# Transposes of the attention stage on 64 lanes at a time, moved in between the third and the last scores

## The chip, the cores and the metric

The kernel runs on one core of a Trainium2 chip. The metric is the device time of one execution in microseconds (us), lower is better. The program of before ran three times; the median of these is the time that the change is compared with. One more execution was taken by the hardware profiler; all views of the trace come from it.

## What is computed

Three stages follow each other, in float32. Attention with a sigmoid in place of the softmax, on 4 x 12 heads of 448 tokens with 64 features; then two MLPs over all 1792 tokens (768 features, 2048 hidden ones), the first with ELU between its products, the second with h - tanh(h).

```python
def _attn_ref(q, k, v):                       # (4, 12, 448, 64) each
    scores = scale * np.matmul(q, k.transpose(0, 1, 3, 2)) - np.log(S)
    attn = 1.0 / (1.0 + np.exp(-scores))
    return np.matmul(attn, v).astype(np.float32)
...
    x = attn_out.transpose(0, 2, 1, 3).reshape(B * S, H * D)
    h = x @ w_in;  g = np.where(h > 0, h, np.exp(np.minimum(h, 0)) - 1);  x = g @ w_out
    h = x @ moe2_w_in;  return (h - np.tanh(h)) @ moe2_w_out
```

The four weights lie in memory as pairs of 32-bit words (float64). They are loaded whole and narrowed on the chip by one ScalarE pass (L538) and two VectorE passes (L541, L545).

## The kernel before

**Stages.** Attention takes about the first 180 us, the two MLPs the rest. The MLPs form their products out of seven block products instead of eight (L743 the first matrix of each MLP, L898 the second); for this the weights need sums of their blocks. The output weights of the first MLP are read, narrowed and summed already during attention, in eight pieces j = 0 to 7 of two 768 KB loads each (`p_load`, L589), which land in two rooms, XA and XB, used in turn by j odd and even; `p_narrow` (L593), `p_sum` (L596) and `p_store` (L600) then take each piece on to a scratch in DRAM, `p_forms`. In the trace of L538 the tile names XA and XB show such a piece. Three quarters of the input weights' pieces are loaded in the same time (`job`, L1030 on).

**Attention.** The 48 heads go in 24 pairs. For a pair n:
- `ld_qk` (L221) loads q and k, `side_by_side` (L226, GpSimd) copies them so that the two heads' features lie side by side in 128 columns. Tokens lie on the partitions (lanes): k in chunks of 128 tokens, q in chunks of 112.
- `transpose(n, w)` (L296) turns the four chunks of k (w=1) and of q (w=0) on TensorE, into the two halves (PSUM banks) of one PSUM tile called `sps`. Features of head 0 then lie on lanes 0 to 63, of head 1 on lanes 64 to 127.
- `head` (L305) copies the turned values to `e`, rounded to fp32r, k on ScalarE, q on VectorE; `rest` (L313, VectorE) writes what the rounding left. Two buffers of `e` (`es`) serve even and odd pairs.
- `scores(n, u)` (L326), u = 0 to 3, are the products for four blocks of key tokens. For u < 3 the two heads run in two halves of the TensorE array, 64 lanes each, six matmuls into one `sps` tile; u = 3 takes 128 lanes at once (both heads' last 64 keys), three matmuls into a tile of its own, `spq`.
- `sig(n, u)` (L346, ScalarE L352) takes the sigmoid of each; `pv(n, u)` (L356, TensorE L363) multiplies by v into `pvps`; `xdone` (L368, VectorE L375) stores the result.

There are three `sps` tiles. Scores u = 0 to 2 of a pair and the transposes for the pair two later share them in rotation: the transposes of pair n + 2 run in the turn of pair n, into the tile that the scores (n, 0) used, so they wait for the sigmoid (n, 0).

**Order.** A scheduler in the kernel (`Sched`) sets the order of every engine. Attention's operations stand at times of a table, `PHASES`, one turn of `CYCLE` = 6900 per pair, and go onto their engines in that order. A first pass plans the operations of attention alone; the second fits all others (narrowing, sums, x forms, here "fill-in work") on ScalarE and VectorE into the gaps: one may start when it ends no more than `GIVE` = 100 ns after the planned start of the next attention operation on its engine. All loads and stores of this stage but a few at the start are issued by one engine, SyncE (SP), in order.

Of the kernel before, what the change touches and what calls it, by code (L numbers as in the profile page):

```python
# [13 lines left out]
ALU = mybir.AluOpType  # L14


class Sched:
# [1 line left out]


    def __init__(self):
        self.ops, self.before, self.plan = {}, {}, {}
# [8 lines left out]
    def emit(self, only_plan=False):  # L31
        ops, plan, late = self.ops, self.plan, 0

        planned = {q: sorted((k for k in plan if ops[k][0] == q), key=plan.get, reverse=True) for q in ("ACT", "DVE")}
        after = {k: [a for a in o[3] if a in ops] for k, o in ops.items()}
        then = {k: [] for k in ops}
        left = {}
        for k, a in after.items():
            a = set(a) | ({self.before[k]} if k in self.before else set())
            left[k] = len(a)  # L40
            for x in a:
                then[x].append(k)
        ready, free, done, order = {}, {}, {}, []
        for k, n in left.items():
            if not n:
                ready.setdefault(ops[k][0], {})[k] = 0
        while any(ready.values()):
            best = None
            for queue, keys in ready.items():
                t0 = free.get(queue, 0)  # L50
                for k, t in keys.items():
                    c = (max(t, t0), ops[k][4], str(k))
                    if k not in plan and planned.get(queue) and c[0] + ops[k][1] > plan[planned[queue][-1]] + late + GIVE:
                        c = (10 ** 9,) + c[1:]
# [12 lines left out]
            for x in then[k]:  # L67
                left[x] -= 1
                if not left[x]:
                    ready.setdefault(ops[x][0], {})[x] = max((done[y] for y in after[x]), default=0)  # L70
        assert len(order) == len(ops)
        if only_plan:
            self.plan = {o[3]: o[0] for o in order}
# [26 lines left out]
def kernel(  # L100
# [20 lines left out]
    nc = tc.nc  # L121
# [3 lines left out]
    R = 4  # L125
# [17 lines left out]
    def f(ap):  # L143
        return ap.bitcast(F32)
# [23 lines left out]
    with tc.manual_schedule():  # L168
# [7 lines left out]
        def attention():  # L176
# [18 lines left out]
                base=0, channel_multiplier=1,  # L195
            )

            DD = 2 * D
            raw_qk = ld_p.tile([128, 4 * NL * R * D], F32, name="raw_qk")

            def parted(t):
                a, b = NL * R * DD, NL * (R + 3) * DD
                return t[:SP, :a], t[:, a:b], t[:, b:b + NL * DD].rearrange("p (i x) -> p i x", i=NL)

            (ql, kl, rest0), (qraw, kraw, rest1) = parted(first), parted(raw_qk)
            krest = rest0, rest1
# [2 lines left out]
            vl = [vs_p.tile([128, NL, 10, D], F32, name=f"vl{i}") for i in range(NVL)]  # L209

            es = [e0, ld_p.tile([128, 4, 512], F32R, name="e1")]
            for i in range(2):
                nc.gpsimd.memset(krest[i][RS:128, :, :D], 0.0)
                nc.gpsimd.memset(krest[i][0:RS, :, D:], 0.0)
# [3 lines left out]

            T = {}

            def ld_qk(w, n):  # L221
                b, hp = pairs[n]
                x = k[b, 2 * hp:2 * hp + 2, 0:384].rearrange("h (p c) d -> p h (c d)", c=3) if w else q[b, 2 * hp:2 * hp + 2].rearrange("h (p r) d -> p h (r d)", r=R)
# [14 lines left out]
            def ld_first(kind, i):  # L238

                b, hp = pairs[i]  # L240
                h = slice(2 * hp, 2 * hp + 2)
                if kind == "k":
                    nc.sync.dma_start(out=kl[:, i].rearrange("p c (h d) -> p c h d", h=2), in_=k[b, h, 0:384].rearrange("h (p c) d -> p c h d", c=3))
                else:
                    (nc.sync if i else nc.scalar).dma_start(out=ql[:, i].rearrange("p c (h d) -> p c h d", h=2), in_=q[b, h].rearrange("h (p r) d -> p r h d", r=R))

            def ld_v(m, i):
                by = nc.sync if m or i else nc.scalar
# [19 lines left out]
            def loads(m):  # L268
# [11 lines left out]
                for x, (kind, args) in enumerate(jobs):  # L280
                    free = {"k": (2, ("t", 1)), "q": (2, ("t", 0)), "v": (NVL, ("pv", 3))}[kind[0]]
                    last = [(free[1][0], NL * (m - free[0]) + i) + free[1][1:] for i in range(NL)]
                    sch.op(
                        ("ld" + kind, m) + args, "SP", 600 * {"kfirst": 1, "qfirst": 1, "kr": 2, "v": 1, "vr": 2}[kind],
                        lambda kind=kind, args=args: kinds[kind](m, *args),
                        last, when("ldv" if kind[0] == "v" else "ldk", NL * m) + x, 2500,
                    )
# [6 lines left out]
                return [part] + ([("ldkr", m)] if kind == "k" else [])  # L294

            def transpose(n, w):  # L296
                if ("tps", n) not in T:
                    T["tps", n] = pss[(4 * n - 5) % 3].tile([128, 2, BK], F32, tag="s", name="sps")
                T["t", n, w] = ps = T["tps", n][:, w]
                P, t = ((SP, ql), (128, kl))[w]  # L300
                for c in range(R):
                    x = krest[n // NL % 2][:, n % NL] if w and c == 3 else t[:, n % NL, c]
                    nc.tensor.transpose(ps[:, c * P:(c + 1) * P], x, ident[:P, :P])  # L303

            def head(n, w):  # L305
                W, slot = ((S, 1), (512, 2))[w]
                to, x = es[n % 2][:, slot, :W], T["t", n, w][:, :W]
                if w:
                    nc.scalar.activation(out=to, in_=x, func=ACTF.Copy)
                else:  # L310
                    nc.vector.tensor_copy(out=to, in_=x)  # L311

            def rest(n, w):  # L313
                W, slot, to = ((S, 1, 0), (512, 2, 3))[w]
                e = es[n % 2]
                nc.vector.tensor_tensor(
                    out=e[:, to, :W], in0=T.pop(("t", n, w))[:, :W], in1=f(e[:, slot, :W]), op=ALU.subtract
                )

            def keep_warm(n):  # L320
# [66 lines left out]
            for n in range(NPR):  # L387
# [4 lines left out]
                used = [("s", n - 2, u) for u in range(4)]  # L392
                for w in (1, 0):
                    if n >= NL:
                        sch.op(("ldqk", n, w), "SP", 600, lambda n=n, w=w: ld_qk(w, n), [("side", n - NL, w)], when("ldqk", n) - w, 5000)
# [16 lines left out]
        def mlp():  # L412
# [617 lines left out]
            def job(key, keeps, place, after=(), only=False, i=0):  # L1030
# [7 lines left out]
                after = list(after) + list(stage_frees[place])  # L1038
                if not live:
                    after.append(("keep", kept_by[key], key))  # L1040
                raw_op(("load", n), "SP", 600, lambda: load(n, key, not live), after, 8500 if place == 4 else 8500 if live else 6000)
                done = ("load", n)
                if place == 4:
                    fixed[done] = 3 * CYCLE + n
# [9 lines left out]
                stage_frees[place] = [done]  # L1054
                if keeps:
                    kept_by[key] = n
                    raw_op(("keep", n, key), "SP", 600, lambda: keep(n, key), [done], 12000 if place == 4 else 5600)
# [319 lines left out]
            for j in range(NG):  # L1377
# [97 lines left out]
```

## Time and profile before

| | us |
|---|---|
| median of three runs (lowest, highest) | 1003.37 (1001.11, 1007.04) |
| profiled execution, its own time | 1005.48 |
| its span in the profile | 1003.70 |
| TensorE busy in the span | 989.4 |
| attention, up to the last turn of pairs | about 180 |

The mean granted clock of TensorE in the profiled execution is 0.996 of full speed. A timeline groups neighbouring instructions of one kind: start, length of the whole group, line, tile, count, and in square brackets the idle time of the engine just before the group and what ended it. Matmuls are pipelined, so a group's length overlaps with the next one's start by some tens of nanoseconds; the distance between starts is the safer number. Lane counts stand as "lanes*columns" of the stationary operand.

### The profile page before, as it was taken

What the parts mean: (1) busy time and instruction counts of PE and PEld (TensorE: products, weight loads), DVE (VectorE), ACT (ScalarE), POOL (GpSimd) and SP (SyncE); (2) the same over time, 40 slices, a digit from 0 to 9 for tenths busy, and PEclk for the clock granted to TensorE, in tenths of its full rate; (3) what the DMA queues carried; (4) which work ended last, traced back from release to release, by engine and by line L of the source; (5) the groups of instructions that cost most, each with busy time, mean ns of one, the idle gap of its engine ahead of it and who ended that gap; (6) DMA issues with size and microseconds to landing.
All of it is one profiled execution on the core that took longest, in us unless ns stands there. A gap on an engine that the chain in (4) does not pass through costs nothing.

```text
span 1003.7 us, 15632 instructions
## 1 busy us (share of the span) xinstructions
PE 989.4 (99%) x5294; PEld 854.3 (85%) x5294; DVE 765.2 (76%) x1155; ACT 600.6 (60%) x966; POOL 105.2 (10%) x118
## 2 busy tenths in 40 slices
PE   8999999999999999999999998999999999999998
PEld 5655565788888888888899987888988999999998
DVE  2798777988888888668887898877777789665673
ACT  4778668766666666656566564444444555446652
POOL 2111210202222220000000201111111000000000
PEclk9999899999999999999999999999999999999999
DMA  8999950155555579999984734555555894455442
GB/s 258 286 356 343 328 180 27 48 192 190 187 188 191 192 254 323 396 364 389 377 284 128 243 90 156 181 196 190 185 188 186 308 330 148 127 170 174 130 144 86
DMA packets 144751, 218.61 MB, mean 218 GB/s; under 512 B 21600, under 2 KB 103072, under 8 KB 144416
## 3 DMA queue, kind: packets, MB, share of 16 engines
q1 hardware_dynamic: 143120, 217.04, 63.8%
q8 instruction: 41, 0.67, 0.3%
q10 hardware_dynamic: 1552, 0.59, 0.2%
q14 instruction: 38, 0.31, 0.1%
HBM read 142.61 MB, written 74.97 MB: 217 GB/s over the span
## 4 chain that ended last, share of the span: by engine, by line
PE 95%; DMA 2%; DVE 1%; ACT 1%; issue 0%; SPq 0%; ACTq 0%; DVEq 0%
PE psa L743 12%; PE psd L743 11%; PE psx L743 10%; PE pvps L363 7%; PE psu L898 7%; PE psw L898 7%; PE psv L898 7%; PE psa L898 6%; PE psb L898 6%; PE psb L743 5%; PE sps L338 5%; PE psy L898 5%; PE psx L898 3%; PE sps L303 2%; PE spq L338 2%; PE psd L898 1%
## 5 line engine op out<-in xcount | busy, mean ns | idle before, releaser
L352 ACT ACTIVATE an<-sps,bias 128x896 f32<-128x896 f32 x72 | 67.5, 1006 | 38.1 <-PE sps L338 38.0
L870 ACT ACTIVATE XB<-t 128x384 fp32r<-128x384 f32 (+1 forms) x111 | 61.9, 562 | 36.5 <-PE psw L898 8.4
L874 DVE TENSOR_TENSOR XB<-t,XB 128x384 fp32r<-128x384 f32 (+1 forms) x111 | 68.1, 624 | 11.4 <-ACT XB L870 11.2
L658 POOL TENSOR_TENSOR second<-second 128x384 f32<-128x384 f32 x15 | 18.9, 1263 | 539.9 <-DMA t<-x_forms 213.5
L363 PE MATMUL pvps<-an,vl 128*64 128x448 f32 x288 | 61.7, 565 | 0.0
L870 ACT ACTIVATE XB<-spare 128x512 fp32r<-128x512 f32 (+1 forms) x72 | 40.9, 573 | 26.4 <-PE psw L898 11.4
L338 PEld LDWEIGHTS sps<-e 64*128 64x128 f32 x432 | 39.7, 190 | 19.7 <-PE pvps L363 15.5
L743 PE MATMUL psa<-XB,W 128*128 128x512 f32 x192 | 54.2, 391 | 0.0
L338 PE MATMUL sps<-e 64*128 64x448 f32 x432 | 52.2, 384 | 0.0
L874 DVE TENSOR_TENSOR XB<-spare,XB 128x512 fp32r<-128x512 f32 (+1 forms) x72 | 44.0, 621 | 7.7 <-ACT XB L870 7.4
L898 PE MATMUL psu<-XB,XB 128*128 128x384 f32 (+1 forms) x192 | 46.3, 348 | 0.0
L898 PE MATMUL psw<-XB,XB 128*128 128x384 f32 (+1 forms) x192 | 46.2, 348 | 0.0
L898 PE MATMUL psv<-XB,XB 128*128 128x384 f32 (+1 forms) x192 | 46.2, 348 | 0.0
L743 PEld LDWEIGHTS psa<-XB,W 128*128 128x128 f32 x192 | 36.0, 188 | 7.6
L363 PEld LDWEIGHTS pvps<-an,vl 128*64 128x64 f32 x288 | 19.0, 140 | 27.3 <-issue 21.0
L772 ACT ACTIVATE spare<-t 128x512 f32<-128x512 f32 (+1 forms) x33 | 19.1, 579 | 37.1 <-DVE t L760 35.9
L658 POOL TENSOR_TENSOR first<-first,second 128x384 f32<-128x384 f32 x30 | 40.0, 1333 | 1.2
L228 POOL COPY first<-raw_qk 128x384 f32<-128x384 f32 (+1 forms) x44 | 26.0, 599 | 122.6 <-DMA raw_qk<-in_k_dram 69.9
L311 DVE CAST e<-sps 128x448 fp32r<-128x448 f32 x24 | 15.0, 625 | 29.7 <-PE sps L303 22.6
L743 PE MATMUL psd<-XB,W 128*128 128x512 f32 x144 | 35.7, 391 | 1.5 <-DVE W L675 1.3
L776 ACT ACTIVATE spare<-spare 128x512 f32<-128x512 f32 (+1 forms) x64 | 36.7, 573 | 0.7
L898 PE MATMUL psa<-XB,XB 128*128 128x384 f32 (+1 forms) x156 | 36.9, 347 | 0.0
(363 smaller groups left out, 2759.1 us busy)
## 6 DMA issues: line engine op xcount, KB each, us to landing
x_forms<-R1b SPq DMA_DIRECT2D x58, 256.0 KB, 2.0
first<-p_forms SPq DMA_DIRECT2D x36, 384.0 KB, 6.6
t<-x_forms SPq DMA_DIRECT2D x64, 192.0 KB, 3.0
t<-x_forms SPq DMA_DIRECT2D x47, 256.0 KB, 4.9
x_forms<-t SPq DMA_DIRECT2D x44, 256.0 KB, 2.0
x_forms<-R1b SPq DMA_DIRECT2D x58, 192.0 KB, 4.9
first<-in_moe_w_in_dram SPq DMA_DIRECT2D x14, 768.0 KB, 5.4
second<-in_moe_w_in_dram SPq DMA_DIRECT2D x14, 768.0 KB, 6.7
```

The lines of the kernel that those rows point to most:

```text
L228: nc.gpsimd.tensor_copy(out=(ql, kl)[w][:, n % NL].rearrange("p c (h d) -> p c h d", h=2), in_=x)
L303: nc.tensor.transpose(ps[:, c * P:(c + 1) * P], x, ident[:P, :P])
L338: nc.tensor.matmul(out=ps[:, j, :S], lhsT=e[lanes, ks, cols], rhs=e[lanes, qs, :S], start=(x == 0), stop=(x == 2),)
L352: nc.scalar.activation(out=a[:, :m], in_=T.pop(("s", n, u))[:, :m, :S], func=ACTF.Sigmoid, bias=bias, scale=scale)
L363: nc.tensor.matmul(out=ps[D * j:D * j + D], lhsT=vl[n // NL % NVL][:, n % NL, 5 * j + u if u < 3 else 3 + j], rhs=a[:, j if u < 3 else 0], ...
L658: by.tensor_tensor(out=out, in0=x, in1=y, op=op)
L743: nc.tensor.matmul(out=ps, lhsT=w[wz][:, k0:k0 + 128], rhs=xs[xz][:, kk], start=(opens and n == 0), stop=(n == 3 * KH - 1), skip_group_che ...
L772: nc.scalar.activation(out=r, in_=h, func=ACTF.Tanh)
L776: nc.scalar.activation(out=r, in_=r, func=ACTF.Exp, scale=-1.0)
L870: nc.scalar.activation(out=at_place(og_place[i, s, p, j], 0, i)[:, :HW[s]], in_=T["graw", i, s, p, j], func=ACTF.Copy)
L874: nc.vector.tensor_tensor(out=lo, in0=T.pop(("graw", i, s, p, j)), in1=f(hi), op=ALU.subtract)
L898: nc.tensor.matmul(out=T["o2", tag], lhsT=lhsT, rhs=rhs, start=(p in OPENS and j == 0 and x == 0), stop=(j == NG - 1 and x == 2), skip_gro ...
```

## The change

The transposes take half of the lanes each: for k two of 64 lanes per chunk, for q two of 56 (at lanes 0 and 64), the two halves into the two PSUM banks; 16 instead of 8 for a pair, each with half as many moving columns. They are emitted between the third scores and the last, not after the last. `head` and `rest` read the turned values by a strided view of the two banks. q is loaded in two transfers per pair, not one, since its tokens now start at lanes 0 and 64, and the GpSimd copy takes 120 lanes. In the scheduler, fill-in work may end later than the next planned operation's start, by 100 ns or 0.4 of that operation's slack; the lateness that it allows for is TensorE's alone. Two rules set when the weights' loads may be issued: piece j of the output weights after the first scores of pair 16 * j // 10 (before: of pair 1 for all), and the input weights' first pieces after scores (0, 1).

```diff
-                    if k not in plan and planned.get(queue) and c[0] + ops[k][1] > plan[planned[queue][-1]] + late + GIVE:
+                    if k not in plan and planned.get(queue) and c[0] + ops[k][1] > self.until[planned[queue][-1]] + late:
...
-                late = start - plan[k]
+                if queue == "PE":
+                    late = start - plan[k]
...
+                last = min([ends[x] - (wait if k in after[x] else cost) for x in then[k]], default=plan[k])
+                ends[k] = plan[k] if ops[k][0] == "PE" else max(plan[k], last)
+            self.until = {k: plan[k] + max(GIVE, int(SLACK * (ends[k] - plan[k]))) for k in plan}
...
+SLACK = 0.4
...
-    ("s", 0): 0, ("s", 1): 620, ("s", 2): 1240, ("s", 3): 1900,
-    ("t", 1): 3100 - 2 * CYCLE, ("t", 0): 3500 - 2 * CYCLE, ("pv", 0): 4000, ("pv", 1): 4900, ("pv", 2): 5800, ("pv", 3): 6500,
+    ("s", 0): 0, ("s", 1): 620, ("s", 2): 1240, ("s", 3): 2400,
+    ("t", 1): 1900 - 2 * CYCLE, ("t", 0): 2100 - 2 * CYCLE, ("pv", 0): 4000, ("pv", 1): 4900, ("pv", 2): 5800, ("pv", 3): 6500,
...
-                nc.sync.dma_start(out=(qraw, kraw)[w][:, n % NL], in_=x)
...
+                for a in range(2):
+                    nc.sync.dma_start(out=qraw[64 * a:64 * a + SH, n % NL], in_=q_rows(b, h, a).rearrange("h (p r) d -> p h (r d)", r=R))
...
-                P, t = ((SP, ql), (128, kl))[w]
+                ps = T["tps", n]
+                P, t, c0 = ((SH, ql, 256), (64, kl, 0))[w]
                 for c in range(R):
                     x = krest[n // NL % 2][:, n % NL] if w and c == 3 else t[:, n % NL, c]
-                    nc.tensor.transpose(ps[:, c * P:(c + 1) * P], x, ident[:P, :P])
+                    for a in range(2):
+                        lanes = slice(64 * a, 64 * a + P)
+                        nc.tensor.transpose(ps[:, a, c0 + c * P:c0 + (c + 1) * P], x[lanes], ident[lanes, lanes])
+                T["t", n, w] = ps[:, :, c0:c0 + R * P].rearrange("p a (c x) -> p c a x", c=R)
...
-                    op("t", n, (w,), "PE", (420, 440)[w], transpose, loaded("qk"[w], n) + before_s(n - 2, 3))
+                    op("t", n, (w,), "PE", (250, 280)[w], transpose, loaded("qk"[w], n) + before_s(n - 2, 3))
...
-                    op("p_load", (j, c), "SP", 600, p_load, [("s", 1, 0)] + (was[c:c + 1] if wide else held), 11000)
+                    op("p_load", (j, c), "SP", 600, p_load, [("s", 0 + 16 * j // 10, 0)] + (was[c:c + 1] if wide else held), 11000)
```

**On TensorE**, one turn in the middle of attention. L338 are the scores (L364 after the change), L303 the transposes (L328), L363 the products with v (L389); e_120 and e_83 are the two buffers of `e`. Before:

```order
L338 MATMUL sps<-e_120 128x448 x18
L338 MATMUL spq<-e_120 128x448 x3
L303 MATMUL sps<-ident,first 128x128 x3
L303 MATMUL sps<-ident,raw_qk 128x128
L303 MATMUL sps<-ident,first 128x112 x4
L363 MATMUL pvps<-an,vl_118 64x448 x6
L363 MATMUL pvps<-a,vl_118 64x448 x2
```

After the change:

```order
L364 MATMUL sps<-e_120 128x448 x18
L328 MATMUL sps<-ident,first 128x64 x6
L328 MATMUL sps<-ident,raw_qk 128x64 x2
L328 MATMUL sps<-ident,first 128x56 x8
L364 MATMUL spq<-e_120 128x448 x3
L389 MATMUL pvps<-an,vl_118 64x448 x6
L389 MATMUL pvps<-a,vl_118 64x448 x2
```

The transposes have moved ahead of the last scores, and there are twice as many with half the columns. The order of the MLPs' instructions is the same on all engines.

**On ScalarE**, the place where piece 5 of the output weights is narrowed (XB_71<-XA_70). L352 are the sigmoids (L378 after), L309 the rounding of k (L337), L709 the forms of x (L735). Before, the last row is the first three sigmoids of pair 12:

```order
L352 ACTIVATE an<-sps,bias 128x896 x3
L352 ACTIVATE a<-spq,bias 128x448
L309 ACTIVATE e_120<-sps 128x512
L538 ACTIVATE XB_71<-XA_70 128x768 x2
L709 ACTIVATE XA<-R0b 128x512
L352 ACTIVATE an<-sps,bias 128x896 x3
```

After the change, the last row is the first three sigmoids of pair 11:

```order
L378 ACTIVATE an<-sps,bias 128x896 x3
L378 ACTIVATE a<-spq,bias 128x448
L337 ACTIVATE e_83<-sps 128x512
L564 ACTIVATE XB_71<-XA_70 128x768 x2
L378 ACTIVATE an<-sps,bias 128x896 x3
```

Piece 5 is narrowed one turn earlier, and a form of x has left that gap. Pieces 4 and 6 move by one turn as well (now ahead of pairs 9 and 13); piece 7 stands ahead of pair 15 in both.

**On SyncE's queue**, around the loads of the same piece (XA_70<-in_moe_w_out_dram; L589, L615 after). L224 loads q and k of a pair (L240 and L243 after), L603 and L629 store sums, L557 keeps a narrowed input weight in DRAM. Before:

```order
L603 DMA p_forms<-XB_71 128x384
L589 DMA XA_70<-in_moe_w_out_dram 128x1536
L557 DMA kept_wi_3_872<-R1b 128x768
L603 DMA p_forms<-XB_71 128x2x384
L233 DMA raw_qk<-in_k_dram 64x2x64 x2
L224 DMA raw_qk<-in_k_dram 128x2x192
L224 DMA raw_qk<-in_q_dram 112x2x256
L589 DMA XA_70<-in_moe_w_out_dram 128x1536
```

After the change:

```order
L273 DMA vl_119<-in_v_dram 128x2x192
L240 DMA raw_qk<-in_k_dram 128x2x192
L629 DMA p_forms<-XB_71 128x2x384
L243 DMA raw_qk<-in_q_dram 56x2x256 x2
L615 DMA XA_70<-in_moe_w_out_dram 128x1536 x2
L629 DMA p_forms<-XB_71 128x4x384
```

The two loads of the piece stand together, and each load of q is two. Up to and with the second of these loads SyncE issues 103 transfers instead of 95, and 26.38 MB instead of 27.26 MB.

## Rows read from the trace of the kernel before

**Rows 1.** The page: busy time of each engine, and its DMA share by slices.
```profile
PE 989.4 (99%) x5294; PEld 854.3 (85%) x5294; DVE 765.2 (76%) x1155; ACT 600.6 (60%) x966; POOL 105.2 (10%) x118
...
DMA  8999950155555579999984734555555894455442
```

**Rows 2.** Timeline of TensorE, one turn with transposes: start, length, instructions.
```profile
66.83 2.09 PE L338 MATMUL sps<-e 64*128 64x448 f32 x18
...
68.56 0.37 PE L338 MATMUL sps<-e 64*128 64x448 f32 x2
...
68.85 0.89 PE L338 MATMUL spq<-e 128*128 128x448 f32 x3
69.59 0.49 PE L303 MATMUL sps<-ident,first 128*128 128x128 f32 x3
...
70.02 0.55 PE L303 MATMUL sps<-ident,first 112*128 112x112 f32 x4
70.50 2.48 PE L363 MATMUL pvps<-an,vl 128*64 128x448 f32 x12
...
73.66 0.47 PE L338 MATMUL sps<-e 64*128 64x448 f32 x2
```

**Rows 3.** Timeline of TensorE, the last turns, which have no transposes.
```profile
167.94 2.09 PE L338 MATMUL sps<-e 64*128 64x448 f32 x18
...
173.93 0.47 PE L338 MATMUL sps<-e 64*128 64x448 f32 x2
```

**Rows 4.** Timeline of ScalarE in the turn of rows 2.
```profile
67.81 2.81 ACT L352 ACTIVATE an<-sps,bias 128x896 f32<-128x896 f32 x3 [0.60 <-PE sps L338]
...
74.63 1.01 ACT L352 ACTIVATE an<-sps,bias 128x896 f32<-128x896 f32 x1 [1.41 <-PE sps L338]
```

**Rows 5.** Timeline of TensorE around its longest stop.
```profile
119.84 1.83 PE L303 MATMUL sps<-ident,first 128*128 128x128 f32 x8 [2.39 <-ACT an L352]
...
127.03 2.09 PE L338 MATMUL sps<-e 64*128 64x448 f32 x18
```

**Rows 6.** Timeline of ScalarE ahead of that stop.
```profile
117.39 0.89 ACT L538 ACTIVATE XB<-XA 128x768 f32<-128x768 f32 x1 [2.87 <-DMA XA<-in_moe_w_out_dram]
118.70 2.79 ACT L352 ACTIVATE an<-sps,bias 128x896 f32<-128x896 f32 x3
```

**Rows 7.** The chain that ended last, from 104 to 119 us: start, length, what.
```profile
108.58 8.73 DMA XA<-in_moe_w_out_dram
```

**Rows 8.** Windows: stretch, length, busy PE, PEld, DVE, ACT, POOL, clock, DMA share, GB/s.
```profile
28.00:32.00 4.00, 4.00 (x27) 2.35 (x27) 1.63 (x3) 3.87 (x6) 0.68 (x2) 1.00 0.77 208
36.00:40.00 4.00, 4.00 (x25) 1.74 (x25) 3.52 (x7) 3.88 (x6) 1.39 (x2) 1.00 0.62 187
60.00:80.00 20.00, 20.00 (x137) 12.19 (x135) 18.07 (x29) 16.63 (x22) 3.49 (x6) 1.00 1.01 340
119.40:126.20 6.80, 6.36 (x22) 3.05 (x24) 2.44 (x4) 3.85 (x6) 2.18 (x4) 0.50 1.03 327
```

**Rows 9.** Weight loads by line and shape: count, busy us, mean ns of one, idle.
```profile
L338 PEld LDWEIGHTS sps<-e 64*128 64x128 f32 x432 | 39.7, 190 | 19.7 <-PE pvps L363 15.5 <-issue 1.3 <-DVE e L316 0.4
...
L338 PEld LDWEIGHTS spq<-e 128*128 128x128 f32 x72 | 11.9, 191 | 8.0 <-issue 7.6
```

**Rows 10.** Timeline of TensorE at the first turn.
```profile
13.04 1.11 PE L338 MATMUL spq<-e 128*128 128x448 f32 x3
...
15.45 0.57 PE L303 MATMUL sps<-ident,first 112*128 112x112 f32 x4 [0.86 <-ACT e L309]
15.96 2.48 PE L363 MATMUL pvps<-an,vl 128*64 128x448 f32 x12
...
19.12 1.08 PE L338 MATMUL sps<-e 64*128 64x448 f32 x8
```

**Rows 11.** Timeline of SyncE's queue: start, time to issue, what.
```profile
70.82 0.38 SPq L224 DMA_DIRECT2D raw_qk<-in_q_dram  x1
...
85.39 0.53 SPq L589 DMA_DIRECT2D XA<-in_moe_w_out_dram  x1
```

**Rows 12.** The load issued at 85.39, by its source line.
```profile
DMA to landing us min/median/max: 7.4/7.4/7.4
```

More of the change, by code (lines that the diff above doesn't have):

```diff
@@ L21, in __init__ @@
     def __init__(self):
-        self.ops, self.before, self.plan = {}, {}, {}
+        self.ops, self.before, self.plan, self.until = {}, {}, {}, {}
     def op(self, key, queue, cost, fn, after, rank, latency=60):
@@ L72, in emit @@
         if only_plan:
-            self.plan = {o[3]: o[0] for o in order}
+            self.plan = plan = {o[3]: o[0] for o in order}
+            ends = {}
+            for _, _, _, k in sorted(order, key=lambda o: o[:2], reverse=True):
+                cost, wait = ops[k][1], ops[k][1] + ops[k][5]
+                last = min([ends[x] - (wait if k in after[x] else cost) for x in then[k]], default=plan[k])
+                ends[k] = plan[k] if ops[k][0] == "PE" else max(plan[k], last)
+            self.until = {k: plan[k] + max(GIVE, int(SLACK * (ends[k] - plan[k]))) for k in plan}
             return
@@ L211, in attention @@
             es = [e0, ld_p.tile([128, 4, 512], F32R, name="e1")]
+            SH = SP // 2
+            nc.gpsimd.memset(qraw[32:64], 0.0)
             for i in range(2):
@@ L219, in attention, with q_rows @@
             T = {}
+            def q_rows(b, h, a):
+                return q[b, h, a * R * SH:(a + 1) * R * SH]
             def ld_qk(w, n):
                 b, hp = pairs[n]
-                x = k[b, 2 * hp:2 * hp + 2, 0:384].rearrange("h (p c) d -> p h (c d)", c=3) if w else q[b, 2 * hp:2 * hp + 2].rearrange("h (p r) d -> p h (r d)", r=R)
-                nc.sync.dma_start(out=(qraw, kraw)[w][:, n % NL], in_=x)
+                h = slice(2 * hp, 2 * hp + 2)
+                if w:
+                    nc.sync.dma_start(out=kraw[:, n % NL], in_=k[b, h, 0:384].rearrange("h (p c) d -> p h (c d)", c=3))
+                    return
+                for a in range(2):
+                    nc.sync.dma_start(out=qraw[64 * a:64 * a + SH, n % NL], in_=q_rows(b, h, a).rearrange("h (p r) d -> p h (r d)", r=R))
             def side_by_side(n, w):
@@ L244, in ld_first @@
                 else:
-                    (nc.sync if i else nc.scalar).dma_start(out=ql[:, i].rearrange("p c (h d) -> p c h d", h=2), in_=q[b, h].rearrange("h (p r) d -> p r h d", r=R))
+                    for a in range(2):
+                        (nc.sync if i else nc.scalar).dma_start(
+                            out=ql[64 * a:64 * a + SH, i].rearrange("p c (h d) -> p c h d", h=2), in_=q_rows(b, h, a).rearrange("h (p r) d -> p r h d", r=R)
+                        )
             def ld_v(m, i):
@@ L298, in transpose, with e_part @@
                     T["tps", n] = pss[(4 * n - 5) % 3].tile([128, 2, BK], F32, tag="s", name="sps")
-                T["t", n, w] = ps = T["tps", n][:, w]
-                P, t = ((SP, ql), (128, kl))[w]
+                ps = T["tps", n]
+                P, t, c0 = ((SH, ql, 256), (64, kl, 0))[w]
                 for c in range(R):
                     x = krest[n // NL % 2][:, n % NL] if w and c == 3 else t[:, n % NL, c]
-                    nc.tensor.transpose(ps[:, c * P:(c + 1) * P], x, ident[:P, :P])
+                    for a in range(2):
+                        lanes = slice(64 * a, 64 * a + P)
+                        nc.tensor.transpose(ps[:, a, c0 + c * P:c0 + (c + 1) * P], x[lanes], ident[lanes, lanes])
+                T["t", n, w] = ps[:, :, c0:c0 + R * P].rearrange("p a (c x) -> p c a x", c=R)
+            def e_part(n, w, slot):
+                return es[n % 2][:, slot, :(S, 512)[w]].rearrange("p (c a x) -> p c a x", c=R, a=2)
             def head(n, w):
-                W, slot = ((S, 1), (512, 2))[w]
-                to, x = es[n % 2][:, slot, :W], T["t", n, w][:, :W]
+                to, x = e_part(n, w, 1 + w), T["t", n, w]
                 if w:
@@ L313, in rest @@
             def rest(n, w):
-                W, slot, to = ((S, 1, 0), (512, 2, 3))[w]
-                e = es[n % 2]
                 nc.vector.tensor_tensor(
-                    out=e[:, to, :W], in0=T.pop(("t", n, w))[:, :W], in1=f(e[:, slot, :W]), op=ALU.subtract
+                    out=e_part(n, w, 3 * w), in0=T.pop(("t", n, w)), in1=f(e_part(n, w, 1 + w)), op=ALU.subtract
                 )
@@ L394, in attention @@
                     if n >= NL:
-                        sch.op(("ldqk", n, w), "SP", 600, lambda n=n, w=w: ld_qk(w, n), [("side", n - NL, w)], when("ldqk", n) - w, 5000)
+                        sch.op(("ldqk", n, w), "SP", 600 * (2 - w), lambda n=n, w=w: ld_qk(w, n), [("side", n - NL, w)], when("ldqk", n) - w, 5000)
                         op("side", n, (w,), "POOL", 1400, side_by_side, [("ldqk", n, w), ("t", n - NL, w)])
-                    op("t", n, (w,), "PE", (420, 440)[w], transpose, loaded("qk"[w], n) + before_s(n - 2, 3))
+                    op("t", n, (w,), "PE", (250, 280)[w], transpose, loaded("qk"[w], n) + before_s(n - 2, 3))
                     op("head", n, (w,), ("DVE", "ACT")[w], (620, 600)[w], head, [("t", n, w)] + used)
@@ L1037, in job @@
                 live = key not in kept_by
-                after = list(after) + list(stage_frees[place])
+                after = list(after) + list(stage_frees[place]) + ([("s", 0, 1)] if place == 4 else [])
                 if not live:
@@ L1056, in job @@
                     kept_by[key] = n
+                    if place == 4:
+                        fixed["keep", n, key] = n * CYCLE
                     raw_op(("keep", n, key), "SP", 600, lambda: keep(n, key), [done], 12000 if place == 4 else 5600)
```

6 lines of the change are left out of this document (3 added, 3 removed).

## The prediction

> **What bounds the kernel.** I read the page first [rows 1]. TensorE is busy 989.4 of 1003.7 us, so only 14.3 us of the span are not matmul, and a change counts by what it takes from TensorE's work or from its waits. The DMA share by slices reads 9 from the second slice to the fifth (25 to 125 us): while attention runs, the transfers are a second full resource. Both matter here.
>
> Then one turn of attention [rows 2]. It lasts 73.66 - 66.83 = 6.83 us with no idle: scores, last scores, transposes, products with v. The last turns have no transposes and last 173.93 - 167.94 = 5.99 us [rows 3], so the transposes of a pair cost 0.84 us, and 22 of the 24 turns have them. TensorE sets the pace: ScalarE sits idle ahead of the turn's first sigmoid, waiting for scores (0.60 and 1.41 us) [rows 4].
>
> The one large stop lies near the end of attention [rows 5]. TensorE stood for 2.39 us at 119.84, waiting for a sigmoid. Behind it is a transfer: ScalarE waited 2.87 us for the last load of output weights, narrowed it at 117.39, and so began the sigmoids of that turn only at 118.70 [rows 6]; the load had been under way from 108.58 to 117.31 [rows 7]. After the stop the granted clock was 0.50 for 6.8 us (1.2 instead of 2.4 GHz) [rows 8]. From the first transpose to the next turn's scores it took 127.03 - 119.84 = 7.19 us, where rows 2 show 73.66 - 69.59 = 4.07: 3.1 us for the clock. The stop cost 2.39 + 3.1 = 5.5 us. So what the change does to the arrival of these loads weighs more than what it does to a transpose.
>
> **The transposes.** In the halves of the array, the 18 score matmuls take 68.85 - 66.83 = 2.02 us, 0.11 each; on 128 lanes three take 69.59 - 68.85 = 0.74, 0.25 each, for the same 448 columns [rows 2]. Halves run side by side there. If the transposes' halves do too, their 0.91 us (69.59 to 70.50) become 0.45. But they now need the turn's own first sigmoid, which frees their PSUM tile, much sooner. Before, they came 2.76 us after the turn's start. That sigmoid starts 67.81 - 66.83 = 0.98 after it, lasts 1.01 [rows 4], and TensorE follows 119.84 - 118.70 - 1.01 = 0.13 later [rows 5, 6]: 2.12, some 0.1 after the third scores are through. Changing from halves to the full array takes about 0.1 (68.56 and a pair's 0.22 leave 0.07 to 68.85). What follows is as in a turn without transposes, 5.99 - 2.02 = 3.97. Sum: 2.12 + 0.45 + 0.1 + 3.97 = **6.65 us a turn, 0.18 less**. Bounds: without the wait and the change of lanes 2.02 + 0.45 + 3.97 = 6.44 (0.39 less); with halves that do not overlap 2.12 + 0.84 + 0.07 + 3.97 = 7.00 (0.17 more). Behind the waiting transposes stand the last scores and the products with v, which no engine needs sooner: ScalarE has two sigmoids to do meanwhile.
>
> What speaks against the halves is the weight load. Each transpose loads 128 columns, now 16 times a turn; a pair of 64-lane score loads occupies 39.7 / 216 = 0.18 us, a load of 128 lanes 11.9 / 72 = 0.17 [rows 9]: half the lanes do not make a load shorter. The trace has no transposes short enough to show how fast loads can follow each other, so I take the overlap and keep 7.00 as the other end. The Trainium skill, TensorE: Matmul & The Clock Gate, section "LDWEIGHTS (loading the stationary operand)", says that a load's time goes by its columns and not by its lanes, P / 1.2 ns. By that, eight pairs of loads of 128 columns are 0.86 us, if the two of a pair run together, and the turn would stay near 7.0; that lanes don't count agrees with rows 9, the figure of one load no row shows.
>
> **The first turn.** Before, the transposes for the third pair waited 0.86 us for `e`, and the first products with v stood behind them, at 15.96 [rows 10]. Now the transposes stand ahead of the last scores: 13.04 + 0.5 + 1.11 gives 14.6 for the products and 17.8 for the second turn, instead of 19.12: **1.3 us sooner**.
>
> **The output weights.** Piece 5 is now narrowed ahead of the sigmoids of pair 11, not of pair 12; its second load was issued at 85.39 and landed 7.4 later, at 92.8 [rows 11, 12]. In the changed order 26.38 MB are issued up to it, not 27.26. At the rate of the full stretch, 340 GB/s [rows 8], 0.88 MB are 2.6 us: 90.2. Two early windows have shares of 0.77 and 0.62 [rows 8]; if the new order fills them, 4 x 0.23 + 4 x 0.38 = 2.4 us more are gained: 87.8. I take the middle, 89.0. With one narrowing (0.89) and the step to the sigmoid these start at 89.95. By TensorE alone they would start at 17.8 + 10 x 6.65 + 0.98 = 85.3. So **a stop of some 4.7 us appears at pair 11**, twice the one of before, and I take it to bring the slow clock again (3.1 us). From there five turns: scores of pair 16 at 89.95 - 0.98 + 5 x 6.65 + 3.1 = 125.3, against 127.03. Piece 7, whose bytes ahead are unchanged, then arrives at 117.3 or earlier, ahead of its sigmoid (89.95 + 4 x 6.65 + 3.1 = 119.65), so the old stop is gone. Gain 1.7 there, and 6 x 0.18 = 1.1 in the turns with transposes that are left: 2.8 us.
>
> **What I cost at nothing.** The strided reads of `head` and `rest`, and the copy with 8 more lanes: their results are needed a turn or more later, and GpSimd is busy 105 us of 1003.7 [rows 1]. If that cover went, a late `e` would show as a TensorE wait for L337 or L339. The fill-in work: what is added to one gap is one narrowing of 0.89, less than the idle 1.41 [rows 4]; uncovered, each would cost its excess directly, since the sigmoid behind it now releases the transposes. The second transfer for q costs SyncE one more issue, 0.38 to 0.53 us [rows 11]; hidden, as the queue is paced by bytes. Uncovered it is the slower rival below. The MLPs' order is the same, so the 2.8 us are carried to the end.
>
> **The sum** is a difference. The profiled execution took 1005.48 us, its span 1003.70 with 1.78 around it, 2.1 above the median of 1003.37. It becomes 1002.7, and the median **1000.6 us**. Some 5 us (0.5%) is about what the measurement can tell from no change.
>
> **Rivals.**
> - *Stop without slow clock.* As forecast, but the clock holds. Scores of pair 16 would come at 122.2, but piece 7 (116 at best, 0.9 to narrow) then holds pair 15 by 0.5: 122.7. Gain 4.3 + 1.1: 998.0. For it: TensorE has other work in a turn. Against: a stop half as long brought the slow clock in rows 5 and 8.
> - *No stop.* The loads of piece 5 land by 84.4. The turns save 1.3 + 21 x 0.18 = 5.1 and the old stop's 5.5 are gone: 992.8. It needs 8.4 us less at landing; I can account for 2.6 and perhaps 2.4.
> - *Halves don't overlap.* The turn is 7.00. Pair 11's sigmoids are due at 17.8 + 70.0 + 0.98 = 88.8, and the stop shrinks to 1.2, too short for the clock. Pair 16 begins at 89.95 - 0.98 + 35.0 = 124.0, 3.0 sooner, and 6 x 0.17 = 1.0 is lost again: 1001.4. So the time alone will not tell this from my forecast. For it: loads, rows 9.
> - *Slower: the queue is paced by transfers, not by bytes.* Up to piece 5 there are twelve more transfers for q (103 in all for 95, as others now come later). Each at 0.38 us, its landing is 90.2 + 12 x 0.38 = 94.8 and the sigmoids start at 95.7; pair 16 then begins 4.0 later than before, less 1.1: 1006.3. At 0.53 us it is 1008.2, 0.5% slower. It loses from 0.14 us per transfer on. For it: SyncE issues in order. Against: the share of 1.01 at 340 GB/s [rows 8] leaves no time in which the transfers' engines wait for issues.
>
> **How the numbers follow.** Chances: forecast 0.36, clock held 0.17, no stop 0.12, no overlap 0.20, slower rival 0.15. Faster than 998.4 are the no-stop case, half of the clock-held one and a part of the forecast where the loads are near 87.8 (0.09): 0.31. Slower than 1008.4 is the slower rival at its upper price and what I have not seen: 0.10. Same: 0.59. The range 993 to 1007 leaves out half of the no-stop case and the upper part of the slower one.
>
> **What would show it.** Transposes (L328) starting about 2.1 us after their turn's scores and taking 0.45; turns of 6.65; the second turn's scores at 17.8. A stop of TensorE near 89 with ScalarE waiting for XA, and a clock near 0.5 behind it; no stop at 117. Wrong if transposes take 0.8, if TensorE waits each turn for a late sigmoid, if piece 5 lands by 84 or after 92, or if the landings run behind with the DMA share below 0.9.

## The result, and the profile after

The changed kernel takes 1008.15 us (median of 20 runs, 1005.05 to 1012.73) against 1003.16 us (20 runs) for the kernel before: a ratio of 1.0054, with a 95% interval of 1.0039 to 1.0069. It is slower by 5 us, and lies 1.15 us beyond the range of the prediction. The profiled execution has a span of 1010.0 us, 6.3 more than before; it took 1011.68 us, 3.5 above the median, so its stops are likely longer than those of most runs.

The page of the changed kernel, engines and DMA share, as in [rows 1]:

```profile
PE 987.0 (98%) x5486; PEld 848.9 (84%) x5486; DVE 768.0 (76%) x1155; ACT 601.8 (60%) x966; POOL 108.9 (11%) x119
...
DMA  7998971055555568999984733555555895455442
```

TensorE has 2.4 us less to do, but it idles for 23 us, not 14.3. And the DMA share reads 7 and 8 in the first and the fourth slice, where before had 8 and 9.

The timeline of TensorE in the changed kernel shows the first turn, an undisturbed one (100.18) and the two long stops, as in [rows 2, 5, 10]:

```profile
14.57 2.48 PE L389 MATMUL pvps<-an,vl 128*64 128x448 f32 x12
...
17.73 0.48 PE L364 MATMUL sps<-e 64*128 64x448 f32 x2
...
73.42 2.09 PE L364 MATMUL sps<-e 64*128 64x448 f32 x18
79.08 0.58 PE L328 MATMUL sps<-ident,first 64*128 64x64 f32 x6 [3.58 <-ACT an L378]
...
81.53 4.52 PE L389 MATMUL pvps<-an,vl 128*64 128x448 f32 x12
...
86.73 2.09 PE L364 MATMUL sps<-e 64*128 64x448 f32 x18
...
100.18 2.09 PE L364 MATMUL sps<-e 64*128 64x448 f32 x18
102.31 0.40 PE L328 MATMUL sps<-ident,first 64*128 64x64 f32 x6
...
102.58 0.43 PE L328 MATMUL sps<-ident,first 56*128 56x56 f32 x8
102.94 0.87 PE L364 MATMUL spq<-e 128*128 128x448 f32 x3
...
106.91 2.09 PE L364 MATMUL sps<-e 64*128 64x448 f32 x18
114.31 0.58 PE L328 MATMUL sps<-ident,first 64*128 64x64 f32 x6 [5.31 <-ACT an L378]
...
121.42 2.12 PE L364 MATMUL sps<-e 64*128 64x448 f32 x18
```

The undisturbed turn is 106.91 - 100.18 = 6.73 us, with transposes 2.13 after its start that take 102.94 - 102.31 = 0.63 up to the last scores. The second turn begins at 17.73, 1.39 sooner than before. All that is close to the forecast. But the turns from 73.42 and from 106.91 last 13.3 and 14.5 us. ScalarE shows why:

```profile
74.83 0.89 ACT L564 ACTIVATE XB<-XB 128x768 f32<-128x768 f32 x1 [3.21 <-DMA XB<-in_moe_w_out_dram]
77.15 0.89 ACT L564 ACTIVATE XB<-XB 128x768 f32<-128x768 f32 x1 [1.43 <-DMA XB<-in_moe_w_out_dram]
77.94 2.79 ACT L378 ACTIVATE an<-sps,bias 128x896 f32<-128x896 f32 x3
...
93.24 0.90 ACT L564 ACTIVATE XB<-XA 128x768 f32<-128x768 f32 x1 [0.76 <-DMA XA<-in_moe_w_out_dram]
94.43 2.81 ACT L378 ACTIVATE an<-sps,bias 128x896 f32<-128x896 f32 x3 [0.29 <-PE sps L364]
...
108.66 0.89 ACT L564 ACTIVATE XB<-XB 128x768 f32<-128x768 f32 x1 [3.55 <-DMA XB<-in_moe_w_out_dram]
112.38 0.89 ACT L564 ACTIVATE XB<-XB 128x768 f32<-128x768 f32 x1 [2.83 <-DMA raw_qk<-in_k_dram]
113.17 2.79 ACT L378 ACTIVATE an<-sps,bias 128x896 f32<-128x896 f32 x3
```

The first two and the last two narrowings are pieces 4 and 6 of the output weights: they wait for loads, and the sigmoids stand behind them, as at the one stop of before [rows 6], now at two. For the narrowing at 112.38 the profile names a load of k, but the piece's own second load landed just then: SyncE's issue at 112.36 had waited for it too.

```profile
SPq L615 <- DMA XB<-in_moe_w_out_dram: 3.3, 1, 3.3
```

The old stop (piece 7) is gone, and piece 5 (93.24) makes none: TensorE, delayed at pair 9, has the scores for the next sigmoids (94.43) ready only after it. Behind both stops the granted clock was 0.50 (columns as in [rows 8]):

```profile
79.10:84.50 5.40, 5.40 (x27) 2.75 (x29) 2.86 (x5) 4.44 (x7) 1.13 (x2) 0.50 0.94 318
114.40:119.40 5.00, 5.00 (x27) 2.67 (x29) 3.53 (x7) 3.27 (x5) 1.72 (x2) 0.50 0.93 311
```

Scores of pair 22 come at 175.20 instead of 167.94, 7.26 later; 1.0 of that is regained in the MLPs.

A window over most of attention, before, after, and for two runs told below. Before:

```profile
20.00:117.00 97.00, 97.00 (x644) 58.09 (x643) 80.19 (x136) 74.36 (x96) 16.04 (x26) 1.00 0.99 331
```

After the change:

```profile
20.00:117.00 97.00, 85.78 (x657) 48.16 (x658) 71.64 (x117) 66.68 (x86) 17.21 (x26) 0.94 0.93 305
```

The kernel before with q in two transfers:

```profile
20.00:117.00 97.00, 93.21 (x602) 54.62 (x602) 76.85 (x127) 71.14 (x93) 17.25 (x25) 0.98 0.93 306
```

The kernel before with the new scheduling rules alone, which has a stop of 4.47 us in this stretch too:

```profile
20.00:117.00 97.00, 92.53 (x600) 55.34 (x602) 82.66 (x135) 73.54 (x95) 19.13 (x28) 0.98 1.00 336
```

The share and the rate (last two numbers) fall by the same amount where q's loads are split, 331 to 305 and 306 GB/s, and not where TensorE only stops. So with q in two the transfers' engines are less busy although there is more to wait for.

### The profile page after: what moved, and what is told of

Same layout as the page of the kernel before. It is cut to its first block, busy times and chain, and to the rows that moved or that the text cites. A ratio compares the mean times of both kernels' runs of the same rounds, so it can differ in the third digit from the quotient of the medians.

```text
span 1010.0 us, 16064 instructions
## 1 busy us (share of the span) xinstructions
PE 987.0 (98%) x5486; PEld 848.9 (84%) x5486; DVE 768.0 (76%) x1155; ACT 601.8 (60%) x966; POOL 108.9 (11%) x119
## 4 chain that ended last, share of the span: by engine, by line
PE 92%; DMA 4%; DVE 1%; ACT 1%; issue 1%; SPq 1%; POOL 0%; ACTq 0%; POOLq 0%; DVEq 0%
PE psa L769 13%; PE psd L769 11%; PE psx L769 10%; PE psu L924 7%; PE psw L924 7%; PE psv L924 7%; PE pvps L389 6%; PE psa L924 6%; PE psb L924 6%; PE psb L769 5%; PE psy L924 4%; PE sps L364 4%; PE psx L924 3%; DMA XB<-in_moe_w_out_dram 2%; PE spq L364 2%; PE sps L328 1%
## 5 line engine op out<-in xcount | busy, mean ns | idle before, releaser
L378 ACT ACTIVATE an<-sps,bias 128x896 f32<-128x896 f32 x72 | 67.5, 1006 | 33.5 <-PE sps L364 33.3
L389 PE MATMUL pvps<-an,vl 128*64 128x448 f32 x288 | 63.0, 575 | 0.0
L364 PEld LDWEIGHTS sps<-e 64*128 64x128 f32 x432 | 40.1, 190 | 18.9 <-PE pvps L389 15.5
L364 PE MATMUL sps<-e 64*128 64x448 f32 x432 | 52.0, 383 | 0.0
L389 PEld LDWEIGHTS pvps<-an,vl 128*64 128x64 f32 x288 | 19.4, 143 | 32.2 <-issue 23.2
L247 POOL COPY first<-raw_qk 128x384 f32<-128x384 f32 (+1 forms) x44 | 28.7, 661 | 126.1 <-DMA raw_qk<-in_k_dram 75.7
L924 PE MATMUL psb<-XB,XB 128*128 128x384 f32 (+1 forms) x156 | 36.8, 347 | 0.0
```

Source lines behind the costliest of these rows:

```text
L247: nc.gpsimd.tensor_copy(out=(ql, kl)[w][:, n % NL].rearrange("p c (h d) -> p c h d", h=2), in_=x)
L364: nc.tensor.matmul(out=ps[:, j, :S], lhsT=e[lanes, ks, cols], rhs=e[lanes, qs, :S], start=(x == 0), stop=(x == 2),)
L378: nc.scalar.activation(out=a[:, :m], in_=T.pop(("s", n, u))[:, :m, :S], func=ACTF.Sigmoid, bias=bias, scale=scale)
L389: nc.tensor.matmul(out=ps[D * j:D * j + D], lhsT=vl[n // NL % NVL][:, n % NL, 5 * j + u if u < 3 else 3 + j], rhs=a[:, j if u < 3 else 0], ...
L924: nc.tensor.matmul(out=T["o2", tag], lhsT=lhsT, rhs=rhs, start=(p in OPENS and j == 0 and x == 0), stop=(j == NG - 1 and x == 2), skip_gro ...
```

## The experiments

Ratios are to the kernel before, run on the same chip, with 95% intervals. Theory A: the new rules place narrowings a turn too early. Theory B: the 22 more transfers for q hold up SyncE's queue.

**The allowance back at 100 ns.**

```diff
-SLACK = 0.4
+SLACK = 0.0
```

> The changed kernel with the fill-in work's allowance back at 100 ns; TensorE's order is that of the changed kernel. Theory A (the narrowings of the output weights stand a turn too early on ScalarE, and the in-order engine holds the sigmoids behind them): piece 4 now stands ahead of pairs 10 and 11 and piece 6 ahead of pairs 14 and 15, so no stop of TensorE over 1 us in attention, turns of 6.72 us, scores of pair 22 at 159 to 161 us instead of 175.2, time 994 to 998 us. Theory B (the 22 additional transfers for q hold up SyncE's queue, and the loads land late wherever they are awaited): landings no sooner than in the changed kernel (piece 4 at 77, piece 6 at 112), stops of 2 to 6 us remain, time 1003 to 1008 us.

Measured: 1007.97 us, 1.0045 (1.0027 to 1.0063). The waits of TensorE in its profile:

```profile
PE psd L769 <- ACT R1b L781: 3.3, 1, 3.3
PE sps L328 <- ACT an L378: 2.7, 1, 2.7
PE sps L328 <- POOL first L247: 2.2, 1, 2.2
```

The stops at pairs 9 and 13 are gone, as A says; others came in their place (a late load of input weights ahead of ScalarE at pair 4, a late load of k with GpSimd's copy behind it at pair 17, and the MLP's first products), and the time is that of the changed kernel. A alone is not the cause.

**Transposes and q loads with all scheduling rules of before** (`Sched`, the gates and the input weights' ranks as in the kernel before).

> The changed transposes and q loads with all scheduling rules of before (allowance, lateness, gates of the weights' loads). Piece 4 stands ahead of pair 10, piece 6 ahead of pair 15. Theory A: stops under 2 us in sum, time 995 to 999 us: the transposes alone are worth 4 to 8 us. Theory B: stops as in the changed kernel, time 1003 to 1008 us.

Measured: 1005.39 us, 1.0030 (1.0011 to 1.0050), the time of B, but not for B's reason. The stops that B expected have not come: in its profile TensorE's waits for a sigmoid are 2.6 us in sum, attention ends 7 us sooner than before (173.0 for 180.0), and 4.9 us are then spent in one wait of the MLP's first products. So this run does not decide between A and B.

**The rules alone**, transposes and q loads as before.

> The kernel before with the new scheduling rules alone; transposes and q loads as before. Pieces 4, 5 and 7 stand one turn sooner on ScalarE than before. Theory A: stops at pairs 9 to 14 of 5 to 12 us in sum with the slow clock behind some, time 1006 to 1012 us. Theory B: no more transfers than before, so no new stops, time 1001 to 1004 us.

Measured: 1005.22 us, 1.0023 (1.0006 to 1.0041). ScalarE at the place where piece 4 is narrowed, and TensorE's first row behind it:

```profile
75.96 0.89 ACT L547 ACTIVATE XB<-XB 128x768 f32<-128x768 f32 x1 [3.52 <-DMA first<-in_k_dram]
77.88 0.89 ACT L547 ACTIVATE XB<-XB 128x768 f32<-128x768 f32 x1 [1.02 <-DMA XB<-in_moe_w_out_dram]
78.66 2.80 ACT L361 ACTIVATE an<-sps,bias 128x896 f32<-128x896 f32 x3
```

```profile
79.81 0.88 PE L312 MATMUL sps<-ident,first 128*128 128x128 f32 x3 [4.47 <-ACT an L361]
```

A stop of 4.47 us at pair 9, with as many transfers as before: A is true too, at some 2 us, less than I gave it (the time lies between the two ranges).

**q in two transfers, nothing else** (56 lanes each, in the kernel before).

```diff
...
-                nc.sync.dma_start(out=(qraw, kraw)[w][:, n % NL], in_=x)
...
+                for a in range(2):
+                    nc.sync.dma_start(out=qraw[56 * a:56 * a + 56, n % NL], in_=q[b, h, 224 * a:224 * a + 224].rearrange("h (p r) d -> p h (r d)", r=R))
```

> The kernel before with each load of q in two transfers of 56 lanes, nothing else moved. Theory A: the queue is paced by bytes, landings move by less than 0.5 us, time 1002 to 1004 us. Theory B: each of the additional transfers delays what is behind it by 0.3 us or more, the stop at 119.8 us grows from 2.4 to 6 us or more, time 1006 to 1009 us.

Measured: 1007.33 us, 1.0046 (1.0030 to 1.0062): nearly the whole loss of the change. TensorE at the old stop, in the turn of pair 15 (4.57 us, where B had 6 or more):

```profile
127.19 1.83 PE L307 MATMUL sps<-ident,first 128*128 128x128 f32 x8 [4.57 <-ACT an L356]
```

The transposes behind the stop start at 127.19, not 119.84 [rows 5]. Up to the load that they wait for, SyncE issues 16 transfers more: 7.35 / 16 = 0.46 us for each. This is one execution, the slowest of the twelve (1011.04), and a stop of 2.62 us at pair 12 lies ahead of that turn. But the second load of piece 5, ahead of both stops, tells the same: SyncE issued it at 91.21, not 85.39 [rows 11], after 13 transfers more, 0.45 us for each. SyncE's queue in the same profile, and the wait that its last row ends:

```profile
91.21 0.36 SPq L593 DMA_DIRECT2D XA<-in_moe_w_out_dram  x1
...
98.76 0.38 SPq L593 DMA_DIRECT2D XB<-in_moe_w_out_dram  x1
99.23 0.40 SPq L607 DMA_DIRECT2D p_forms<-XB  x1
100.54 0.33 SPq L593 DMA_DIRECT2D XB<-in_moe_w_out_dram  x1
101.05 1.68 SPq L237 DMA_DIRECT2D first<-in_k_dram  x2
102.82 0.58 SPq L225 DMA_DIRECT2D raw_qk<-in_k_dram  x1
103.49 1.31 SPq L228 DMA_DIRECT2D raw_qk<-in_q_dram  x2
106.36 0.40 SPq L255 DMA_DIRECT2D vl<-in_v_dram  x1
```

```profile
SPq L255 <- DMA XB<-in_moe_w_out_dram: 4.5, 3, 1.5
```

The load of v (L255) waits from 104.80 to 106.36 for a load of weights (L593), with which it has no data in common: the one issued at 98.76, eight transfers before it. This is so throughout: from 20 to 117 us all of SyncE's waits for a transfer, 28 before and 29 here, end with the landing of the transfer eight before, and before never more than eight were under way. A half load of q takes a place as a 768 KB load does. In the stretch of 97 us SyncE issued 107 transfers instead of 101 (6% more), of 277 KB in the mean instead of 317 (13% less): so 8% fewer bytes.

**The second half on GpSimd's queue**, in the kernel before with q in two:

```diff
-                    nc.sync.dma_start(out=qraw[56 * a:56 * a + 56, n % NL], in_=q[b, h, 224 * a:224 * a + 224].rearrange("h (p r) d -> p h (r d)", r=R))
+                    (nc.gpsimd if a else nc.sync).dma_start(out=qraw[56 * a:56 * a + 56, n % NL], in_=q[b, h, 224 * a:224 * a + 224].rearrange("h (p r) d -> p h (r d)", r=R))
```

> The kernel before with q in two transfers (as in the run of that name), the second issued by GpSimd on its own queue, so that SyncE issues as many transfers as before. Theory B1 (SyncE's queue is the limit: it keeps eight transfers in flight, and each small one takes a place that a large one would have): the 4 us come back, time 1002 to 1005 us, DMA share 20 to 117 us at 0.98 or more. Theory B2 (transfers of 56 lanes are slow in themselves): time 1006 to 1008 us as with both on SyncE.

Measured: 1001.71 us, 0.9986 (0.9967 to 1.0005), against 1.0046 with both on SyncE. The same transfers, the same shapes, another queue: B1. Its profile is again of the slowest run (1008.53); there the share is 0.97 at 323 GB/s, just short of the 0.98 that I had named, and a stop of 3.6 us is left.

**The same edit in the changed kernel.**

> The changed kernel, the second half of each q load issued by GpSimd. Theory B1: the stops of 10.9 us shrink to 5 us or less, time 1001 to 1005 us, 3 us or more below the changed kernel. Theory B2: 1007 to 1009 us as it is. Theory A (the narrowings' place alone makes the stops): 1006 to 1009 us, with stops at pairs 9 and 13.

Measured: 1003.18 us, 0.9999 (0.9983 to 1.0015), against 1.0054. The window over attention:

```profile
20.00:117.00 97.00, 93.11 (x730) 51.66 (x728) 81.69 (x131) 73.81 (x95) 28.59 (x42) 0.98 1.00 327
```

The loss of the change is gone, but no gain has come.

**The opposite of the change: fewer transfers on SyncE.** In the kernel before, `ld_kr` (two 32 KB loads per two pairs) goes to GpSimd.

```diff
-                    nc.sync.dma_start(
+                    nc.gpsimd.dma_start(
                         out=krest[m % 2][RS * j:RS * j + RS, :, D * j:D * j + D],
...
```

> The kernel before with the two 32 KB loads of k's last rows per two pairs issued by GpSimd: SyncE has one transfer per pair less, the opposite of what the change does. Theory B1: loads land sooner by 0.3 us per transfer that is gone, the stop at 119.8 us is gone or under 1 us, time 997 to 1001 us. Theory B2: bytes and shapes are the same, time 1002 to 1005 us.

Measured: 1001.50 us, 0.9981 (0.9966 to 0.9996), and the twelve runs lie between 1000.6 and 1002.0, where the kernel before spreads over 9 us. Its profile has no stop at 119.8. It has one of 2.4 at the start, for k's first rows, and the time is half a us above B1's range.

**Old rules, second half on GpSimd.**

> The changed transposes with all scheduling rules of before, the second half of each q load issued by GpSimd. Theory B1: attention's stops under 1.5 us, attention ends by 172 us; what is left of the gain is decided where the MLP begins and VectorE still forms x (a stop of 4.95 us there in the run with both halves on SyncE): time 1001 to 1004 us. Theory B2: 1004 to 1007 us.

Measured: 1003.19 us, 0.9997 (0.9980 to 1.0014), with 4.9 us again at the MLP's first products.

**The changed kernel with both on GpSimd** (second half of q and `ld_kr`).

> The changed kernel with the second half of each q load and the two 32 KB loads of k's last rows issued by GpSimd: SyncE has one transfer per pair less than in the kernel before. Theory B1 alone: no stop over 1 us, turns of 6.72 us throughout, attention ends at 171 to 172 us against 176.3 for the kernel before with the same loads moved (1001.5 us); time 996 to 998 us unless VectorE is late at the MLP's first products. Theory A (the early narrowings matter besides): stops of 3 us or more at pairs 9 to 13 remain, time 1000 to 1004 us.

Measured: 1000.89 us, 0.9990 (0.9969 to 1.0010). The profile, of its slowest run, still has stops of 1.3 and 3.6 at pairs 11 and 13, as A says, and 3.1 at the start.

**The same with the transposes back behind the last scores** (still in halves; `PHASES` of before).

> As the run before, but the transposes (in halves) stand after the last scores, as in the kernel before, where their PSUM tile has long been freed. If the place between third and last scores costs its wait for the sigmoid and a change of lanes: turns of 6.45 to 6.55 us instead of 6.72, attention 4 to 5 us shorter where nothing stops it. If the place costs nothing: turns of 6.7 us or more. Time 994 to 1001 us, decided by the weights' loads and by VectorE at the MLP's start.

Measured: 999.82 us, 0.9974 (0.9952 to 0.9995). Turns are 6.62 us, between the two cases that I had named: the place that the change chose costs 0.10 a turn.

**The changed kernel with both on GpSimd and the allowance at 100 ns.**

> The changed kernel with fill-in work's allowance back at 100 ns and the same loads on GpSimd. Theory A: narrowings stand one to two turns later, so no stop in attention at all, but the forms of x are behind and VectorE holds up the MLP's first products by 3 to 5 us, as in the two runs with late fill-in work: attention ends at 171 us, time 1000 to 1003 us. If the allowance makes no difference once the queue is relieved: time within 1.5 us of the run with the allowance at 0.4.

Measured: 1003.25 us, 1.0002 (0.9980 to 1.0024): no stop in attention behind the start, 3.2 us at the first products. With the queue relieved the allowance of 0.4 is worth 2.4 us (1000.89); with q's second half on SyncE it made no difference that can be told (1.0054 with it, 1.0045 without).

**The best version**: halves behind the last scores, second half of q and `ld_kr` on GpSimd, k's first rows on SyncE.

> The version with the transposes in halves after the last scores, the second half of q and k's last rows on GpSimd's queue, except k's first load, which goes back to SyncE since TensorE waited 3.0 us for it at the start. If those 3 us are carried: time 996 to 998 us. If the weights' loads take them back in new stops: 999 to 1001 us.

Measured: 997.93 us, 0.9956 (0.9935 to 0.9976). One of its turns:

```profile
53.06 2.09 PE L364 MATMUL sps<-e 64*128 64x448 f32 x18
55.08 0.88 PE L364 MATMUL spq<-e 128*128 128x448 f32 x3
55.89 0.71 PE L328 MATMUL sps<-ident,first 64*128 64x64 f32 x16
56.53 2.48 PE L389 MATMUL pvps<-an,vl 128*64 128x448 f32 x12
...
59.69 0.67 PE L364 MATMUL sps<-e 64*128 64x448 f32 x4
```

The transposes take 56.53 - 55.89 = 0.64 here, where they took 0.91 [rows 2].

**The kernel before with the same relief and nothing of the change.**

> The kernel before with k's last rows on GpSimd's queue, the first on SyncE: the same relief without the change. If transposes in halves and the new rules are worth what the turns show (6.62 instead of 6.83 us, 22 times, and 1.3 us at the start), this lies 3 us or more above the version with them (999 to 1001 us); if they are given back elsewhere, within 1.5 us of it.

Measured: 998.61 us, 0.9963 (0.9943 to 0.9984), 0.7 us from the best version, less than the intervals can tell from nothing. In its profile attention ends at 173.2, in the best version's at 173.0: there the 21 shorter turns save 4.2, but the second turn starts at 19.96, not 17.98, and two stops of 0.9 have come at pairs 13 and 15.

**The best version with the scheduling rules of before.**

> As the first of these three, but with all scheduling rules of before: the halves alone, with the queue relieved. If the new rules matter once the queue is relieved (VectorE late at the MLP's first products without them): 2 us or more above the first, with a wait of 3 us or more at the first products. If not: within 1.5 us of it.

Measured: 1005.05 us, 1.0028 (1.0010 to 1.0047). Its longest wait, and VectorE (third busy number) in the window around it:

```profile
PE psd L768 <- ACT R1b L780: 7.2, 1, 7.2
```

```profile
192.50:200.00 7.50, 0.38 (x3) 0.05 (x1) 7.50 (x16) 4.28 (x9) 0.00 (x0) 0.76 0.19 71
```

VectorE is busy without a gap while TensorE waits 7.2 us: I read this as fill-in work (the forms of x) left over from attention's shorter turns.

## Why the prediction was wrong

**The step that failed** is the one that costs q's second transfer at nothing, "hidden, as the queue is paced by bytes". I read it from a DMA share of 1.01 at 340 GB/s. That row shows that the transfers' engines were full with the transfers of then, not that smaller ones would keep them full. The queue was paced by number as well: each further transfer delayed the piece behind it by about 0.46 us where it was tried alone, near the 0.38 of the slower rival. The rival's mechanism is what happened, though at other pieces than its sum says: it would have passed 0.5% at 0.53 us per transfer with one stop; here it came with two stops and the slow clock behind both. The forecast's own term shows it as well: the second load of piece 5, which I had at 89.0 and the rival at 94.8, was narrowed from 93.24 (the stop at pair 9 has a part in that). And between 80 and 100 us the share was below the 0.9 that I had named as a sign of landings that run behind:

```profile
80.00:100.00 20.00, 19.91 (x129) 9.98 (x126) 15.03 (x24) 14.97 (x21) 4.10 (x6) 0.86 0.87 281
```

**The stops.** That loads of output weights would hold the sigmoids and bring the slow clock was right, and so was that the old stop at piece 7 would go. But I worked out piece 5 alone, though pieces 4 and 6 had moved one turn as well. They made the stops: the turns of pairs 9 and 13 took 6.6 and 7.8 us more than 6.7. With 1.9 for two small stops (pairs 4 and 8) that is 16.3, where before lost 5.65. Less 1.4 at the start and 20 turns of 0.10, it gives the 7.3 us by which pair 22 is late.

**The turn.** The halves do run side by side, so the rival without overlap fell: in the changed kernel four pairs of k's halves take 102.58 - 102.31 = 0.27 us from start to start, where four whole ones took 70.02 - 69.59 = 0.43 [rows 2]; halves that run one after the other, twice as many with half the columns, would take about as long as the whole ones. An estimate from the figure of the Trainium skill, TensorE: Matmul & The Clock Gate, section "LDWEIGHTS (loading the stationary operand)", gives a pair's loads of 128 columns 0.107 even if the two run together, 0.43 for four pairs; the trace does not agree. The wait for the sigmoid (2.13, forecast 2.12) was right. Only the change of lanes and the tail were too low (0.63 from the first transpose to the last scores, where I had 0.55), so a turn is 6.72 to 6.73, not 6.65. The first turn was right to 0.1 us.

**Nothing lost at the MLP** was right for this kernel (1.0 us regained), but by the new allowance alone: with the old rules the shorter turns lose 3 to 7 us there to VectorE.

What the three parts are worth, by single runs with the rest as before: q's second transfer 0.46%, the rules 0.23%, and transposes in their new place -0.16% (the run with old rules less the one with q alone). The sum, 0.53%, is the change's 0.54%, but each part is known to some 0.2% only and depends on the others, so that it fits so well is luck: moving q's second half to GpSimd takes 0.60% off in the kernel before, 0.55% in the changed one and 0.33% under the old rules, and in the best version the new rules save 0.72% instead of costing 0.23%.

That places in flight, rather than the time to issue, set the 0.46 us was argued from SyncE's waits and not tried: GpSimd's queue relieves both. What speaks for it is that issuing leaves SyncE time: its rows add up to 58.2 of the 97 us before and to 59.8 with q in two.

One slip in the forecast's chances: 0.12, half of 0.17 and 0.09 make 0.30 for a faster result, not 0.31.

## What to carry to other kernels

When a queue feeds transfer engines that are full, count its transfers and not only their bytes: splitting one load in two can cost more than the engine work that it saves, and moving small loads to an idle engine's queue may be worth more than the edit. Ask of each resource that is nearly full (here TensorE, SyncE's queue, VectorE) what it does when the first gets faster; a gain of 4 us in turns ended as 0.7 us, no more than noise. And where a schedule moves several pieces by a turn, work out all of them.

## What the hardware showed unexpectedly

Sixteen transposes of 64 or 56 lanes run in 0.64 us where eight of twice the lanes took 0.91: not half. k's first rows, loaded by GpSimd at the start, held TensorE for 3.0 us, which the same loads on SyncE did not; in the changed kernel with both on GpSimd it issued them only at 4.30, after the buffers that it fills first. The kernel before spreads over 9 us from run to run; with k's last rows on GpSimd over 1.3 (2.8 with the first of them on SyncE). The spread goes with the clock: in the 35 runs of the kernel before that stand beside the first four experiments, the five with a mean granted clock of 1.000 took 997.8 to 1000.4 us, the ten at 0.996 or below 1000.5 to 1007.2. So the stop with its slow clock, which the prediction read from one profile, is likely not in every run (the only profile of that kernel has it), and the relief may gain mostly by keeping it away.
